# Transposes moved ahead of the first layer's matmuls, and row statistics a slot later, in an attention and MLP kernel

## The chip, the cores and the metric

The kernel runs on one core of a Trainium2 chip. The metric is the device time of one execution in microseconds. Before the change the median of three runs was 1268.01 us (1264.45 to 1271.99).

## The reference

Batch 8, 8 heads, 576 tokens, head size 64; then a two-layer perceptron of width 2048 on the 512 joined features, with layer norm and a residual.

```python
scores = scale * np.matmul(q, k.transpose(0, 1, 3, 2))      # 8 x 8 heads, 576 x 576
cum = np.cumsum(np.log(np.clip(f, 0.0001, 1.0)), axis=-1)
decay = cum[:, :, :, None] - cum[:, :, None, :]
scores = np.where(causal, -1e9, scores + decay)
attn = np.exp(scores - np.max(scores, axis=-1, keepdims=True))
attn = attn / (np.sum(attn, axis=-1, keepdims=True) + 1e-09)
x = heads_joined(np.matmul(attn, v))                        # (8, 576, 512)
xn = (x - mean(x)) / np.sqrt(var(x) + 1e-06) * g_ln
out = x + np.maximum(xn @ w_ch1, 0.0) @ w_ch2
```

## The kernel before, in words

All 64 heads are done one after the other, each in four slots, and the layers run beside them. A head's 576 query rows are cut into row tiles 0 to 4 (64 rows, then four of 128, table `QT`); the slots of a head are t = 1, 2, 3, 4, and slot t=1 does row tile 0 too. Row tile t needs 192, 320, 448 and 576 keys. There are 256 slots, numbered u. Products are made of values split into a high and a low part (names `h`/`hi` and `l`/`lo`) so that float32 accuracy comes from the fast matmul format.

In a slot the work of several stages meets, and each stage is a piece named by one letter. The string of letters in `ORDERS` is the order in which the pieces' instructions are issued; each engine runs its own instructions strictly in that order, and so does each DMA queue. The pieces that matter here:

- Q (`qk_mm`): TensorE makes the scores of row tile t, tiles `s`.
- S (`softmax_a`, L409): VectorE adds the mask and takes the row maximum, `s` to `p`. e (`softmax_e`, L420): ScalarE, exponential with row sums. B (`softmax_b`): VectorE adds and inverts the sums (L425, L426), POOL scales the rows (L427), and a DMA on SP's queue (L440) writes them to a tile `pw` of the fast format.
- t (`transpose_unit`, L446): two slots later (`LAG`) TensorE transposes `pw` into PSUM tiles `tr` (and `tr_4b` for the last columns of row tile 4). So slot t=1 transposes row tile 3 of the head before, t=2 its row tile 4, t=3 row tiles 0 and 1 of the own head, t=4 row tile 2.
- h (`transposed_hi`, L504): ScalarE copies `tr` to the high part `ph`. l (`transposed_lo`, L509): VectorE makes the low part (the instructions read `tr` and `ph`; the tile written is `pl`, or `ph` in its upper half).
- A (`av_unit`, L543): in slots t=1 and t=3, TensorE makes the product with v, tile `o`, from the `ph` and `pl` of the three slots before; the last of them were written in the slot just before. F (`finish`, L579) and a (`finish_add`, L590) take `o` out of PSUM; ScalarE does F ahead of e.
- M (`Moe.first`, `mm1`, L622 to L624): twelve matmuls of 256 columns, one sixteenth (step j) of the first layer for a chunk of 256 tokens, tile `h`. r (`mm1_high`, L630): relu on ScalarE, tile `hh`. m (`mm1_low`, L635): the low part on VectorE. N (`Moe.second`, `mm2`, L644 to L646): six matmuls of 512 columns, the second layer for the step of the slot before, into `acc`. After the last step N also calls `chunk_out` (L703, L705), which needs `rs`.
- R (`Moe.rest`): after steps j=11 and j=13 `chunk_rows` transposes 128 tokens' rows into a PSUM tile `xp`, copies them to `xt` (L669, ScalarE) and takes their mean and variance (L674, L675, VectorE); after steps 9 and 11 `rows_load` reads such rows, tile `xw`, with 4 to 8 DMAs on SP; `fetch` loads and splits the next chunk's inputs (`xr`, `x`; L655, L606, L607).
- L (`run_later`): up to six of the 14 POOL instructions by which `chunk_rstd` makes `rs`.
- P (`prep`): the next head's casts on ScalarE (L342, L348), VectorE (L349, L356) and POOL (L343, L350, L357), and the load of v (L332). D (`next_raw`): the load of a later head (L325).

All tiles of TensorE's output but `acc` take turns in six PSUM banks (`bank`). After the last slot a loop does M, r, m, L, N, R for the remaining steps alone (the tail). The third table rules slots 66 and later, the second slots 37 to 65.

Of the kernel before, what the change touches and what calls it, by code (L numbers as in the profile page):

```python
# [19 lines left out]
FT = DFF // P  # L20
# [27 lines left out]

ORDERS = [
    (0, "WwQsSthAeMrgFBmlLNPaRf"),  # L50
    (37, "WwQSstAMhPelgNFrfmBDLRa"),
    (66, "QSAFeMaBPrthNmlRLD"),
]


# [1 line left out]
def attn_moe(ctx: ExitStack, tc: tile.TileContext, qk, v, f, g, w1, w2, out):  # L57
# [13 lines left out]
    def bank(name):  # L71
        return ps.tile([P, 512], F32, tag="b", bufs=6, name=name)

    def m2(name, dt):
        return work.tile([P, 512], dt, tag="m2", bufs=11, name=name)
# [340 lines left out]
    def softmax_e(h, t):  # L416
        q0, m, w = QT[t]
        pt, st = h.p[t]
        i = len(h.s[t]) - 1
        nc.scalar.activation(pt[:m, :w], pt[:m, :w], AF.Exp, bias=st[:m, i : i + 1], scale=-1.0, accum_out=st[:m, 2:3])  # L420
# [22 lines left out]
    def tr(out_, in_):  # L443
        m = in_.shape[0]
        if in_.dtype == F32R:
            nc.tensor.transpose(out_.bitcast(F32R), in_, identr[:m, :m])  # L446
        else:
            nc.tensor.transpose(out_, in_, ident[:m, :m])
# [53 lines left out]
    def transposed_hi(h, t):  # L502
        for tp, hi, lo in h.parts:
            nc.scalar.copy(out=hi, in_=tp)  # L504

    def transposed_lo(h):
        if not h.full:
            for tp, hi, lo in h.parts:
                nc.vector.tensor_tensor(out=lo, in0=tp, in1=hi.bitcast(F32), op=ALU.subtract)  # L509
# [100 lines left out]
    def new_chunk(n):  # L610
        c = Chunk()
        c.n, c.x, c.xr, c.xt, c.j = n, [], [], [], 0
        c.acc = None
        return c

    def mm1(c):
# [41 lines left out]
    def rows_load(c, i):  # L658
        c.xw = m2(f"xw{c.n}_{i}", F32R).rearrange("p (k c) -> p k c", k=KT)
        for k in range(KT):  # L660
            tokens(c, k, c.n * C + P * i, P, c.xw[:, k, :].bitcast(F32))

    def chunk_rows(c, i):

        tp = bank(f"xp{c.n}_{i}")
        for k in range(KT):
            tr(tp[:, P * k : P * k + P], c.xw[:, k, :])
        xt = m2(f"xt{c.n}_{i}", F32)
        nc.scalar.copy(out=xt, in_=tp)  # L669
        if i == 0:  # L670
            c.sv = work.tile([P, 2, 2], F32, tag="sv", bufs=2, name=f"sv{c.n}")
            c.rs = work.tile([P, 4], F32, tag="rs", bufs=2, name=f"rs{c.n}")
        bs = work.tile([P, 6], F32, tag="bs", bufs=2, name=f"bs{c.n}_{i}")
        nc.vector.bn_stats(bs, xt)  # L674
        nc.vector.bn_aggr(c.sv[:, i, :], bs)  # L675
        c.xt.append(xt)

    later = []

    def run_later(k):  # L680
        while later and k > 0:
            later.pop(0)()
            k -= 1

    def chunk_rstd(c):

        var, y, t = c.sv[:, :, 1], c.rs[:, 0:2], c.rs[:, 2:4]
        ve = nc.gpsimd
        later.append(lambda: ve.tensor_scalar_add(var, var, 1e-6))
        later.append(lambda: ve.tensor_scalar(  # L690
            out=y.bitcast(I32), in0=var.bitcast(I32), scalar1=-0.5, scalar2=1597463007.0, op0=ALU.mult, op1=ALU.add
        ))
        for _ in range(3):
            later.append(lambda: ve.tensor_mul(t, y, y))
            later.append(lambda: ve.tensor_mul(t, t, var))
            later.append(lambda: ve.tensor_scalar(out=t, in0=t, scalar1=-0.5, scalar2=1.5, op0=ALU.mult, op1=ALU.add))
            later.append(lambda: ve.tensor_mul(y, y, t))
# [9 lines left out]
    class Moe:  # L707
# [49 lines left out]
        def rest(self):  # L757
            c, self.step = self.step, None
            if c is not None:
                self.prev = (c, c.pend)  # L760
                if c.j in (FT - 5, FT - 3):
                    chunk_rows(c, (c.j - (FT - 5)) // 2)
                if c.j in (FT - 7, FT - 5):
                    rows_load(c, (c.j - (FT - 7)) // 2)
                if c.j == FT - 3:
                    chunk_rstd(c)
            self.fetch()

        def left(self):
# [2 lines left out]
    moe = Moe()  # L772
# [7 lines left out]
    def start_head(n):  # L780
        hd[n] = load(n)
# [11 lines left out]
    for u, slot in enumerate(slots):  # L793

        def before(k):
            return slots[u - k] if u >= k else None

        if slot is not None:
            n, t = slot
            h = hd[n]  # L800
        av = None
        if before(LAG + 1) is not None and before(LAG + 1)[1] in (2, 4):
            av = hd[before(LAG + 1)[0]]
        want = moe.can(wp.ready()) and u >= FIRST_MOE

        def piece(c):
            tu = before(LAG)
            if c == "t" and tu is not None:
                transpose_unit(hd[tu[0]], tu[1])
            elif c == "h" and tu is not None:  # L810
                transposed_hi(hd[tu[0]], tu[1])
            elif c == "l" and tu is not None:
                transposed_lo(hd[tu[0]])
            elif c == "Q" and slot is not None:
                if t == 1:
                    qk_mm(h, 0)
                qk_mm(h, t)
            elif c == "A" and av is not None:
                av_unit(av, before(LAG + 1)[1])
            elif c == "S" and slot is not None:  # L820
                if t == 1:
                    softmax_a(h, 0)
                softmax_a(h, t)
            elif c == "e" and slot is not None:
                if t == 1:
                    softmax_e(h, 0)
                softmax_e(h, t)
            elif c in FILL:
                wp.fill(FILL[c])
            elif c == "s":  # L830
                wp.sums()
                if u == LAG:
                    busy(WARM[2])
            elif c == "F" and av is not None:
                finish(av)
            elif c == "a" and av is not None:
                finish_add(av)
            elif c == "r" and want:
                moe.first_high()
            elif c == "R":  # L840
                moe.limit = min(NCHUNK, max(0, u - LAG - 1) // (4 * H) * S // C)
                moe.rest()
            elif c == "L":
                run_later(RSTD)
            elif c == "M" and want:
                moe.first()
            elif c == "B" and slot is not None:
                if t == 1:
                    softmax_b(h, 0)
                softmax_b(h, t)  # L850
            elif c == "m" and want:
                moe.first_low()
            elif c == "W":
                due = 1 + min(u, W_CHANGE) / W_SLOTS + max(0, u - W_CHANGE) * W_TICKS
                while not wp.done() and wp.tick_no <= due:
                    wp.tick()
            elif c == "N":
                moe.second()
            elif c == "P":
                prep()  # L860
            elif c == "D":
                next_raw()

        def next_raw():

            if slot is not None and t in (2, 3) and NFULL <= n + 2 < B * H:
                if t == 2:
                    start_head(n + 2)
                load_raw(hd[n + 2], 1 if t == 2 else 0)

        def prep():

            if slot is not None:
                if t == 1 and n + 1 < NFULL:
                    start_head(n + 1)
                if n == NFULL - 2 and t == 1:
                    while not wp.done():
                        wp.tick()
                        wp.fill(99)
                    early.close()  # L880
                    pools["late"] = ctx.enter_context(tc.tile_pool(name="late", bufs=1))
                if n + 1 >= NFULL and n + 1 < B * H:
                    if t == 2:
                        prep_a(hd[n + 1])
                    if t == 3:
                        prep_b(hd[n + 1])
                if not h.full and t == LAG + 1:
                    prep_v(h)
                if t == LAG + 1 and n + 1 < B * H:
                    load_v(hd[n + 1])  # L890

        for c in [o for first, o in ORDERS if first <= u][-1]:
            piece(c)
    moe.limit = NCHUNK
    while moe.left() > 0 or moe.prev is not None:
        if moe.can(2 * FT):
            moe.first()
            moe.first_high()
            moe.first_low()
        run_later(RSTD)  # L900
        moe.second()
        moe.rest()
# [38 lines left out]
```

## Time and profile before

| | before |
|---|---|
| median of three runs | 1268.01 us |
| profiled execution | 1266.57 us |
| its span | 1264.8 us |
| mean granted TensorE clock | 0.991 |
| matmuls / other matmul-engine instructions | 8368 / 8368 |
| HBM read, written | 79.61 MB, 19.17 MB |

The span is the time from the first to the last instruction of one execution. Busy times are of single engines and overlap. The ends of matmuls are modelled, so that a matmul's duration includes its way through the array; how fast matmuls follow one another is read from their starts. In rows of the timeline the first number is the start from the span's begin and the second the duration, both in us; a bracket gives idle time of the engine just before and what ended it. In rows of DMA issues the last number is the median time in us from issue to landing.

### The profile page before, as it was taken

Reading aid. Unit: us, or ns where it says so; the run is one execution under the profiler, and the core shown is the slowest. Engines: PE = TensorE matmul, PEld = TensorE weight load, DVE = VectorE, ACT = ScalarE, POOL = GpSimd, SP = SyncE. Lnnn points to the kernel's source line nnn. Section 1 sums busy time; section 2 is a strip of 40 time slices with the busy share of each in tenths; the row PEclk is TensorE's granted clock in tenths of the full one; section 3 lists DMA queues with packets and bytes.
Section 4 is the critical chain, followed back from the end, with each engine's and each line's share of the span. In section 5 each row is a group of like instructions: output and inputs, shape, how many; then the busy total and the mean of one; then the engine's idle time right before and its main releaser. Section 6 shows DMA issues by size and latency. Waiting matters only on the chain.

```text
span 1264.8 us, 26082 instructions
## 1 busy us (share of the span) xinstructions
PE 1208.8 (96%) x8368; PEld 1076.5 (85%) x8368; DVE 755.6 (60%) x2664; ACT 621.9 (49%) x1936; POOL 445.6 (35%) x768
## 2 busy tenths in 40 slices
PE   8889999989899999999999999998999999999998
PEld 6657877879788888889898989887888989999997
DVE  6778773566666767676667666766766662222222
ACT  5887674545545555555555555554555542112111
POOL 3544353344434434344434344444334330000000
PEclk8999999999999999999999999999999999999999
DMA  6555442333434343434433434433343421110100
GB/s 173 155 152 167 134 112 69 100 124 120 128 124 121 125 132 117 137 126 118 133 125 128 124 129 127 136 111 114 126 120 123 141 82 39 41 44 17 51 26 26
DMA packets 129657, 139.04 MB, mean 110 GB/s; under 512 B 34544, under 2 KB 102128, under 8 KB 129520
## 3 DMA queue, kind: packets, MB, share of 16 engines
q1 hardware_dynamic: 129520, 137.37, 35.6%
q8 instruction: 67, 1.10, 0.4%
q14 instruction: 70, 0.57, 0.2%
HBM read 79.61 MB, written 19.17 MB: 78 GB/s over the span
## 4 chain that ended last, share of the span: by engine, by line
PE 67%; DVE 13%; ACT 9%; issue 4%; DMA 4%; SPq 2%; POOL 1%; DVEq 0%; POOLq 0%; ACTq 0%
PE h L622 9%; PE acc L644 8%; PE h L623 8%; PE h L624 8%; PE acc L645 8%; PE acc L646 8%; PE o L543 5%; ACT p L420 4%; DVE p L409 4%; PE tr L446 2%; PE s L374 2%; DMA pw<-p 2%; PE o L518 2%; PE s L376 2%; PE s L377 2%
## 5 line engine op out<-in xcount | busy, mean ns | idle before, releaser
L427 POOL TENSOR_SCALAR p<-p,st 64x64 f32<-64x64 f32 (+4 forms) x320 | 173.7, 544 | 542.0 <-ACT p L420 193.4
L622 PE MATMUL h<-x,w1h 128*128 128x256 f32 x1152 | 334.1, 290 | 0.4 <-DVE st L409 0.4
L623 PE MATMUL h<-x,w1h 128*128 128x256 f32 x1152 | 326.9, 284 | 0.0
L624 PE MATMUL h<-x,w1l 128*128 128x256 f32 x1152 | 326.4, 283 | 0.0
L420 ACT ACTIVATE p<-p,st 64x64 f32<-64x64 f32 (+4 forms) x320 | 179.1, 560 | 211.4 <-DVE st L409 209.2
L635 DVE SCALAR_TENSOR_TENSOR hh<-h,hh 128x256 fp32r<-128x256 f32 x288 | 121.3, 421 | 209.4 <-ACT hh L630 206.6
L644 PE MATMUL acc<-w2h,hh 128*128 128x512 f32 x576 | 242.2, 420 | 0.0
L646 PE MATMUL acc<-w2h,hh 128*128 128x512 f32 x576 | 226.6, 393 | 0.0
L645 PE MATMUL acc<-w2l,hh 128*128 128x512 f32 x576 | 226.5, 393 | 0.0
L622 PEld LDWEIGHTS h<-x,w1h 128*128 128x128 f32 x1152 | 220.2, 191 | 5.6 <-issue 0.9
L623 PEld LDWEIGHTS h<-x,w1h 128*128 128x128 f32 x1152 | 220.9, 192 | 2.5
L624 PEld LDWEIGHTS h<-x,w1l 128*128 128x128 f32 x1152 | 221.0, 192 | 0.0
L630 ACT ACTIVATE hh<-h 128x256 fp32r<-128x256 f32 x288 | 109.1, 379 | 181.7 <-PE h L624 178.2
L409 DVE CUSTOM_DVE_ANT_0 p<-s,mask 64x64 f32<-64x64 f32 (+4 forms) x320 | 133.1, 424 | 19.2 <-PE s L377 5.6
L646 PEld LDWEIGHTS acc<-w2h,hh 128*128 128x128 f32 x576 | 108.3, 188 | 25.4
L425 DVE TENSOR_SCALAR st<-st 128x1 f32<-128x1 f32 (+1 forms) x320 | 47.8, 149 | 122.0 <-ACT p L420 118.3
L644 PEld LDWEIGHTS acc<-w2h,hh 128*128 128x128 f32 x576 | 108.6, 189 | 13.7 <-ACT ph_full L504 0.2
L645 PEld LDWEIGHTS acc<-w2l,hh 128*128 128x128 f32 x576 | 109.4, 190 | 12.6
L504 ACT CAST ph<-tr 64x128 fp32r<-64x128 f32 (+4 forms) x384 | 107.2, 329 | 0.2
L579 ACT COPY ot<-o 64x320 f32<-64x320 f32 x96 | 38.0, 396 | 129.5 <-PE o L543 129.2
L543 PEld LDWEIGHTS o<-ph,vv 128*128 128x128 f32 x384 | 54.4, 188 | 44.2 <-DVE ph L509 26.9
L543 PE MATMUL o<-ph,vv 128*128 128x256 f32 (+2 forms) x384 | 61.4, 281 | 31.0 <-DVE ph L509 31.0
(89 smaller groups left out, 1928.5 us busy)
## 6 DMA issues: line engine op xcount, KB each, us to landing
raw<-in_qk_dram SPq DMA_DIRECT2D x96, 288.0 KB, 2.9
wr<-in_w_dram SPq DMA_DIRECT2D x32, 512.0 KB, 5.2
pw<-p SPq DMA_DIRECT2D x48, 288.0 KB, 3.2
pw<-p SPq DMA_DIRECT2D x48, 224.0 KB, 2.2
vr<-in_v_dram SPq DMA_DIRECT2D x64, 160.0 KB, 2.2
out_dram<-xt SPq DMA_DIRECT2D x36, 256.0 KB, 2.1
pw<-p SPq DMA_DIRECT2D x48, 160.0 KB, 2.1
xa<-xs SPq DMA_DIRECT2D x32, 160.0 KB, 1.8
```

The source lines that it names most:

```text
L409: nc.vector.tensor_tensor_reduce(out=pt[:m, a:z], in0=sp, in1=mask[:m, off + a : off + z], scale=-SCALE, scalar=3.0e38 if i == 0 else st[: ...
L420: nc.scalar.activation(pt[:m, :w], pt[:m, :w], AF.Exp, bias=st[:m, i : i + 1], scale=-1.0, accum_out=st[:m, 2:3])
L427: nc.gpsimd.tensor_scalar(out=pt[:m, :w], in0=pt[:m, :w], scalar1=st[:m, 3:4], scalar2=1.0, op0=ALU.mult, op1=ALU.mult)
L543: mm(o, st, mv, start=first, stop=True, skip_group_check=True)
L622: mm(ph, w1h[:, k, fs], c.x[k][:, 0, :], start=(k == 0), stop=False)
L623: mm(ph, w1h[:, k, fs], c.x[k][:, 1, :], start=False, stop=False)
L624: mm(ph, w1l[:, k, fs], c.x[k][:, 0, :], start=False, stop=(k == KT - 1))
L630: nc.scalar.activation(h[:, 0, :], c.ph, AF.Relu)
L635: nc.vector.scalar_tensor_tensor(out=h[:, 1, :], in0=ph, scalar=0.0, in1=h[:, 0, :].bitcast(F32), op0=ALU.max, op1=ALU.subtract)
L644: mm(c.acc[i], h[:, 0, ts_], w2h[:, j, :], start=(j == 0), stop=False)
L645: mm(c.acc[i], h[:, 0, ts_], w2l[:, j, :], start=False, stop=False)
L646: mm(c.acc[i], h[:, 1, ts_], w2h[:, j, :], start=False, stop=(j == FT - 1))
```

## The change

The third table moves t ahead of M, h ahead of P and r, and l ahead of P and m. m stands ahead of N instead of behind. The copy of `xp` and the statistics become a piece of their own, b (`rows_stats`): in the third table it stands behind m and N and ahead of R, so it works on the rows that R transposed a slot before; in the second table it stands behind R, in the same slot. `chunk_rstd` is called by it after the second half of the rows. In the tail b stands ahead of L.

```diff
     (0, "WwQsSthAeMrgFBmlLNPaRf"),
-    (37, "WwQSstAMhPelgNFrfmBDLRa"),
-    (66, "QSAFeMaBPrthNmlRLD"),
+    (37, "WwQSstAMhPelgNFrfmBDLRba"),
+    (66, "QSAFteahBlMPrmNbRLD"),
...
         for k in range(KT):
             tr(tp[:, P * k : P * k + P], c.xw[:, k, :])
+        c.rows = (i, tp)
+
+    def rows_stats(c):
+        if c is None or c.rows is None:
+            return
+        i, tp = c.rows
+        c.rows = None
         xt = m2(f"xt{c.n}_{i}", F32)
         nc.scalar.copy(out=xt, in_=tp)
...
         nc.vector.bn_stats(bs, xt)
         nc.vector.bn_aggr(c.sv[:, i, :], bs)
         c.xt.append(xt)
+        if i == 1:
+            chunk_rstd(c)
...
-                if c.j == FT - 3:
-                    chunk_rstd(c)
...
+            elif c == "b":
+                rows_stats(moe.cur)
...
             moe.first_low()
+        rows_stats(moe.cur)
         run_later(RSTD)
```

TensorE in a slot t=2 of head 22: the last matmul of M, the transposes of row tile 4, and N. Before:

```order
L624 MATMUL h_13_4451<-x_3_3611,w1l 128x256
L446 MATMUL tr_4_4476<-identr,pw_4_4344 64x128
L446 MATMUL tr_4_4476<-identr,pw_4_4344 128x128 x3
L446 MATMUL tr_4b<-identr,pw_4_4344 128x128
L644 MATMUL acc_0_3725<-w2h,hh_12_4408 128x512
L645 MATMUL acc_0_3725<-w2l,hh_12_4408 128x512
```

The same slot now, from Q (tile `s`):

```order
L376 MATMUL s_2_0_4433<-hi_4207 128x320
L377 MATMUL s_2_0_4433<-kl_4208,xq_2727 128x320
L446 MATMUL tr_4_4439<-identr,pw_4_4330 64x128
L446 MATMUL tr_4_4439<-identr,pw_4_4330 128x128 x3
L446 MATMUL tr_4b<-identr,pw_4_4330 128x128
L622 MATMUL h_13_4458<-x_0_3151,w1h 128x256
```

The transposes stand right behind Q, and the twelve matmuls of M behind them, so a transpose that waits holds up M and N.

ScalarE in a slot t=2 of head 29: exponential (L420), the cast of the next head's keys (L342), relu (L630) and the copies of the transposes (L504). Before:

```order
L420 ACTIVATE p_2_6188,st_2_6189<-p_2_6188,st_2_6189 128x320
L342 CAST hi_6210<-raw_1_5990 128x576
L630 ACTIVATE hh_9_6215<-h_9_6192 128x256
L504 CAST ph_28_6156<-tr_4_6217 64x128
L504 CAST ph_28_6156<-tr_4_6217 128x3x128
L504 CAST ph_28_6156<-tr_4b 128x128
```

The same slot now:

```order
L420 ACTIVATE p_2_6188,st_2_6189<-p_2_6188,st_2_6189 128x320
L504 CAST ph_28_6129<-tr_4_6191 64x128
L504 CAST ph_28_6129<-tr_4_6191 128x3x128
L504 CAST ph_28_6129<-tr_4b 128x128
L342 CAST hi_6223<-raw_1_5990 128x576
L630 ACTIVATE hh_9_6228<-h_9_6210 128x256
```

The copies went from behind the cast and the relu to right behind the exponential.

VectorE around the slot t=4 that follows, where rows of tokens had been transposed at the end of t=3: the statistics (BN_STATS, BN_AGGR), S (L409), B (L425, L426), m (L635) and l (L509). Before:

```order
L674 BN_STATS bs_0_6320<-xt_0_6316 128x6
L675 BN_AGGR sv_6318<-bs_0_6320 128x2
L409 ISA p_4_6339,st_4_6340<-s_4_0_6333,mask 128x288
L409 ISA st_4_6340 128x1
L409 ISA p_4_6339,st_4_6340<-s_4_1_6336,mask,st_4_6340 128x288
L409 ISA st_4_6340 128x1
L425 TENSOR_SCALAR st_4_6340<-st_4_6340 128x1
L426 RECIPROCAL st_4_6340<-st_4_6340 128x1
L635 SCALAR_TENSOR_TENSOR hh_11_6362<-h_11_6344,hh_11_6362 128x256
L509 TENSOR_TENSOR ph_29_6294<-tr_2_6364,ph_29_6294 64x128
L509 TENSOR_TENSOR pl_29_6295<-tr_2_6364,ph_29_6294 128x256
```

The same slot now:

```order
L409 ISA p_4_6332,st_4_6333<-s_4_0_6326,mask 128x288
L409 ISA st_4_6333 128x1
L409 ISA p_4_6332,st_4_6333<-s_4_1_6329,mask,st_4_6333 128x288
L409 ISA st_4_6333 128x1
L425 TENSOR_SCALAR st_4_6333<-st_4_6333 128x1
L426 RECIPROCAL st_4_6333<-st_4_6333 128x1
L509 TENSOR_TENSOR ph_29_6264<-tr_2_6336,ph_29_6264 64x128
L509 TENSOR_TENSOR pl_29_6265<-tr_2_6336,ph_29_6264 128x256
L635 SCALAR_TENSOR_TENSOR hh_11_6363<-h_11_6350,hh_11_6363 128x256
L681 BN_STATS bs_0_6376<-xt_0_6372 128x6
L682 BN_AGGR sv_6374<-bs_0_6376 128x2
```

The statistics went from the head of the slot's list to its end, and l from behind m to ahead of it.

More of the change, by code (lines that the diff above doesn't have):

```diff
@@ L612, in new_chunk @@
         c.n, c.x, c.xr, c.xt, c.j = n, [], [], [], 0
-        c.acc = None
+        c.acc = c.rows = None
         return c
```

## Prediction

> **What bounds the kernel now.** I read the page, then the busy time by stretch, then the waits by engine inside the long stretch, then the chain and the timeline at single waits. The page's first part names the engine:
>
> ```profile
> PE 1208.8 (96%) x8368; PEld 1076.5 (85%) x8368; DVE 755.6 (60%) x2664; ACT 621.9 (49%) x1936; POOL 445.6 (35%) x768
> ```
>
> The stretches (busy time of each engine, then granted clock, DMA share, GB/s) part the slots that the third order table rules (243 to 1062 us) from the tail, which holds only the layers:
>
> ```profile
> 243.00:1062.00 819.00, 785.46 (x5524) 716.17 (x5523) 543.54 (x1956) 424.46 (x1347) 329.67 (x540) 1.00 0.39 122
> 1062.00:1264.80 202.80, 198.97 (x1282) 180.17 (x1280) 49.52 (x113) 36.24 (x93) 13.71 (x70) 1.00 0.11 32
> ```
>
> TensorE is the bound in both, at a granted clock of 1.00. In the middle it is idle 819.0 - 785.5 = 33.5 us, and the waits in that stretch (total, times, longest) say for what:
>
> ```profile
> PE o L543 <- DVE ph L509: 31.0, 39, 2.4
> ...
> POOL sv L689 <- DVE sv L675: 37.2, 12, 4.3
> ```
>
> Nearly all of it is one wait: piece A, the product with v, waits for piece l, the low halves of the transposed weights, which VectorE made last in the slot before. (The second row counts chunks: 12 have their statistics in this stretch.) One such wait in the timeline, in a slot t=2 and the A of the slot t=3 behind it:
>
> ```profile
> 602.30 0.70 DVE L674 BATCH_NORM_STATS2 bs<-xt 128x6 f32<-128x512 f32 x1 [0.90 <-ACT xt L669]
> ...
> 604.19 0.19 ACT L420 ACTIVATION_READ_ACCUMULATOR p<-p,st 128x1 f32 x1
> 604.28 0.66 ACT L342 CAST hi<-raw 128x576 fp32r<-128x576 f32 x1
> ...
> 604.59 0.17 DVE L426 RECIPROCAL st<-st 128x1 f32<-128x1 f32 x1
> ...
> 604.84 0.37 ACT L630 ACTIVATE hh<-h 128x256 fp32r<-128x256 f32 x1
> ...
> 605.12 0.62 ACT L504 CAST ph<-tr 64x128 fp32r<-64x128 f32 x2
> 605.25 0.43 DVE L635 SCALAR_TENSOR_TENSOR hh<-h,hh 128x256 fp32r<-128x256 f32 x1 [0.49 <-ACT hh L630]
> 605.29 0.37 PE L377 MATMUL s<-kl,xq 66*128 66x448 f32 x1
> ...
> 605.77 0.28 DVE L509 TENSOR_TENSOR ph<-tr,ph 64x128 fp32r<-64x128 f32 x1
> 606.09 0.56 DVE L509 TENSOR_TENSOR pl<-tr,ph 128x384 fp32r<-128x384 f32 x1
> 606.11 0.80 PE L543 MATMUL o<-ph,vv 128*128 128x256 f32 x5 [0.45 <-DVE ph L509]
> ```
>
> After the exponential (ends 604.38) ScalarE casts the next head's keys, then the relu, then the transposes (605.12); VectorE makes hh's low half first (605.25) and l from 605.77. A starts at 606.11. The bracket says 0.45, but ends on TensorE are modelled: a product of 448 columns hands over after 0.2 us where nothing waits, so A was due at 605.5 and lost 0.6. From starts, not brackets, I make the 39 waits 37 us (0.16 more each), and take 37, with 31 as the lower end.
>
> **The change, part by part.**
>
> *t ahead of M, h ahead of casts and relu, l ahead of the casts and m.* No instruction is added. In the event above B ends at 604.76; l's three instructions (the two shown and 0.28 for tr_4b) would run from there to 605.9, its first done at 605.04, half a microsecond before A is due; the h that they read follows the exponential at 604.38 and takes 0.62 + 0.27. The other A slot, t=1, follows t=4, whose exponential is the longest:
>
> ```profile
> 712.12 0.78 ACT L420 ACTIVATE p<-p,st 128x576 f32<-128x576 f32 x1 [2.04 <-DVE st L409]
> ...
> 713.21 0.17 DVE L426 RECIPROCAL st<-st 128x1 f32<-128x1 f32 x1
> ...
> 714.48 0.51 PE L543 MATMUL o<-ph,vv 128*128 128x320 f32 x3
> ```
>
> l would run from 713.38 for 0.28 + 0.42, to 714.1, and A is due at 714.48: cover 0.4. So this wait goes: **-37 us** (ends -31 and -37). What takes its place in l's old room is m, now last on VectorE: it has until N of the next slot, behind Q, A, t and M, over 2 us. The cast of the next head's keys and the relu on ScalarE come 0.5 to 0.9 us later, by the h rows; the POOL subtraction behind the cast has an idle POOL (35%) after it.
>
> *Junctions of short and long matmuls.* The first long matmul behind a row of short ones loses some time:
>
> ```profile
> 711.01 0.28 PE L622 MATMUL h<-x,w1h 128*128 128x256 f32 x1
> 711.13 0.29 PE L623 MATMUL h<-x,w1h 128*128 128x256 f32 x1
> ...
> 712.45 0.37 PE L446 MATMUL tr<-identr,pw 128*64 128x128 f32 x3
> 712.65 0.46 PE L644 MATMUL acc<-w2h,hh 128*128 128x512 f32 x1
> 712.96 0.39 PE L645 MATMUL acc<-w2l,hh 128*128 128x512 f32 x1
> 713.19 0.40 PE L646 MATMUL acc<-w2h,hh 128*128 128x512 f32 x1
> ...
> 715.02 0.33 PE L622 MATMUL h<-x,w1h 128*128 128x256 f32 x1
> 715.18 0.28 PE L623 MATMUL h<-x,w1h 128*128 128x256 f32 x1
> ...
> 719.98 0.46 PE L446 MATMUL tr<-identr,pw 128*64 128x128 f32 x4
> ```
>
> Behind transposes N's first step is 0.31 instead of 0.23 (0.08 lost); behind A, M's first is 0.16 instead of 0.12 (0.04); behind Q nothing. Before, a slot with A pays both; after, t stands between A and M, so one loss of 0.08 is left: 0.04 to 0.05 in some 85 slots with A, **-4 us** (ends 0 and -9: no loss left at all in those slots).
>
> The Trainium skill, page "TensorE: Matmul & The Clock Gate", section "Back-to-back issue gap", speaks against that term: it gives about 81 ns for each sustained matmul of 128 columns with its own weights, so a longer row of short ones would cost more and the loss is not paid once a row. By it, three or four more short matmuls in the row, each 20 ns over the shortest spacing, would take the 4 us away. The trace gives 65 to 75 ns here (three transposes from 712.45 to 712.65, four in 0.30), between the two.
>
> *What the transposes now wait for.* t reads pw, which a DMA on SP brings two slots after Q. Moved ahead of M it is due 712.45 - 711.01 = 1.44 us sooner, and in t=1 the removed wait of A brings it nearer still. Shortest of the four is row tile 4, transposed in slot t=2:
>
> ```profile
> pw<-p SPq DMA_DIRECT2D x48, 288.0 KB, 3.2
> ```
>
> Landing takes 3.2 us by that row. In an ordinary head:
>
> ```profile
> 714.41 0.47 SPq L440 DMA_DIRECT2D pw<-p  x1
> ```
>
> The issue follows POOL's row, which hangs on Q through S, e and B, all in their old order; it lands at 717.6, and t came at 719.98: spare 2.4, after the change 0.9. But once a chunk rows_load puts its reads into SP's queue ahead of it:
>
> ```profile
> 594.18 0.33 SPq L332 DMA_DIRECT2D vr<-in_v_dram  x1
> 594.61 0.71 SPq L655 DMA_DIRECT2D xw<-xb  x1
> ...
> 597.30 0.56 PE L543 MATMUL o<-ph,vv 128*128 128x320 f32 x3 [0.62 <-DVE ph L509]
> ...
> 599.69 0.47 SPq L440 DMA_DIRECT2D pw<-p  x1
> ...
> 603.23 0.46 PE L446 MATMUL tr<-identr,pw 128*64 128x128 f32 x4
> ```
>
> From 594.61 to 599.69 SP issues eleven DMAs of some 0.45 us. pw lands at 602.9, t came at 603.23: spare 0.3. After, with 1.44 and A's own 0.78 gone, TensorE waits 1.9 us there, with M and N queued behind t. I did this for all 48 heads: issue, plus 3.2, against t's start, less 1.44 and less the A wait between. Ten are short, by 15.8 us together (first and last below; with each DMA's own landing instead of 3.2 it is 12 heads and 19.8):
>
> ```profile
> 258.43 0.47 SPq L440 DMA_DIRECT2D pw<-p  x1
> ...
> 264.06 0.46 PE L446 MATMUL tr<-identr,pw 128*64 128x128 f32 x4
> ...
> 1007.03 0.47 SPq L440 DMA_DIRECT2D pw<-p  x1
> ...
> 1011.85 0.46 PE L446 MATMUL tr<-identr,pw 128*64 128x128 f32 x4
> ```
>
> I take **+18 us**. The ends: +5 if SP's queue itself clears sooner and only the shift by M counts, +20 by the landings.
>
> *Statistics a slot later.* Before, the copy of xp waits for the transposes at the slot's end and the statistics for the copy (0.90 in the row of 602.30); S of the next slot stands behind. After, both inputs are long there; 0.9 us a time on VectorE, off the path once l is early, so 0. The price is PSUM: xp's bank is held until ScalarE has made the next slot's relu (0.37 above) and the copy. The rows show no such wait. Both run beside N (six steps of 0.23, 1.4 us), so the bank is free about when that slot ends; were they half a microsecond late and the bank wanted at once, 24 places would cost 12 us, and nothing where one of the other five banks is next. That is the nearer case, since a slot takes about four: 0. chunk_rstd starts a slot later, so two of its 14 POOL instructions run only when chunk_out asks; chunk_out then waits for POOL once a chunk, but m and l stand ahead of it now: 0. The second table only moves the copy behind rest in the same slot, and the tail's TensorE has 3.8 us idle in all: 0 for both.
>
> **Sum.** -37 - 4 + 18 = -23 on the profiled execution's 1266.6 (span 1264.8 and 1.8 around it): 1243.6. The median of the runs shown is 1.4 higher, so I say **1245 us**.
>
> **The rivals.**
> - *The transposes take what A gave up twice over (slower).* Place: t in slot t=2, every head, not ten. The landings of pw reach far in this stretch:
>
> ```profile
> DMA to landing us min/median/max: 1.7/2.2/4.8
> ```
>
> At 4.8 instead of 3.2 the ordinary spare of 0.9 turns into a wait of 0.7; 48 heads make 32, and the sum is +9: 1277. It decides from about 1.4 us later than now ((23 / 48) + 0.9). Against it: issue there follows Q, S, e, B, whose order stays. Chance 0.09.
> - *The wait of A stays in part (no change).* Cover for l is 0.4 to 0.5 us. If S, e and B run 0.65 later than in the rows, as they may with m and the statistics ahead of S, some 83 A's wait 0.2 each, 17 us, and the sum is -6: 1262. For it: VectorE is busy 66% there. Chance 0.15.
> - *The queue clears and nothing replaces the wait (faster still).* -37 - 4 + 5 = -36: 1232. For it: S of row tile 4 no longer stands behind statistics. Against: POOL had its row done before SP issued it, so SP is the limit. Chance 0.24.
> - The forecast, 1236 to 1256, has 0.52.
>
> The range reaches from the full gain to the partial one, 1230 to 1265. About 0.5%, 6.3 us, is what a measurement of this kernel can tell from no change. Faster 0.52 + 0.24 = 0.76, same 0.15, slower 0.09.
>
> **What would show it.** Right: A's wait for ph falls under 8 us; t (L446) waits for pw some 15 to 20 us in about a dozen places, one a chunk, always ahead of tr_4b, with xw reads ahead of pw in SP's queue; N's first step is 0.23 and M's first behind t near 0.2; the tail is as long as before. Wrong: A still waits for DVE; t waits in most heads; TensorE waits for a bank after xp; or ScalarE's later relu makes N wait.

## The result, and the profile after

The changed kernel took 1252.91 us (median of 4 runs, 1250.83 to 1254.38) against 1267.25 us for the kernel before on the same chip: a ratio of 0.9882, 95% interval 0.9847 to 0.9917. The forecast was 1245 us in a range of 1230 to 1265, so the way and the range held and the gain came out at about three fifths of what was forecast (14 us instead of 23). Run again beside other kernels it gave 0.9884 (0.9856 to 0.9913). One of the six executions of the kernel with one read of rows, below, took 6478.84 us and is left out of that kernel's numbers.

The waits of TensorE in the long stretch of the changed kernel (total, times, longest), where before A's wait stood with 31.0:

```profile
PE tr L446 <- DMA pw<-p: 18.2, 14, 2.6
PE h L622 <- DVE pl L509: 5.3, 4, 1.3
PE o L543 <- DVE ph L509: 1.5, 4, 0.4
```

A's wait is gone, t's wait for pw is there at the size forecast, and a third one, M for l, was not forecast. Stretches from the same place in the program (from the scores of row tile 3 of head 16, the first slot of the third table, to the last matmul of A; then the rest), first before, then after:

```profile
228.94:1047.00 818.06, 784.52 (x5533) 715.27 (x5531) 548.62 (x1980) 428.02 (x1360) 334.90 (x548) 1.00 0.39 123
1047.00:1264.80 217.80, 213.97 (x1381) 193.83 (x1379) 52.73 (x121) 39.42 (x101) 13.71 (x70) 1.00 0.13 35
```

```profile
231.74:1031.26 799.52, 774.08 (x5532) 709.78 (x5531) 540.98 (x1980) 427.52 (x1360) 342.09 (x548) 1.00 0.40 126
1031.26:1249.10 217.84, 213.98 (x1381) 193.85 (x1379) 52.74 (x121) 38.42 (x101) 13.61 (x70) 1.00 0.12 35
```

The tail is unchanged (217.8), the long stretch is 18.5 us shorter, and the stretch ahead of it 2.8 us longer in this execution. Of these 2.8 us, 2.3 are not the change's work: up to the first M the two programs issue the same, and that M starts at 109.0 us before and at 111.3 after. In six executions that differ in the third table alone the stretch ahead was 227.8 to 231.9 us long.

One place where t waits, in a slot t=2 of the changed kernel, in rows of SP, TensorE and VectorE:

```profile
587.89 0.33 SPq L332 DMA_DIRECT2D vr<-in_v_dram  x1
588.28 0.42 SPq L655 DMA_DIRECT2D xw<-xb  x1
...
592.12 0.38 SPq L655 DMA_DIRECT2D xr<-xa  x1
592.59 0.38 SPq L325 DMA_DIRECT2D raw<-in_qk_dram  x1
593.07 0.47 SPq L440 DMA_DIRECT2D pw<-p  x1
```

```profile
594.30 0.31 PE L377 MATMUL s<-kl,xq 66*128 66x320 f32 x1
596.86 0.48 PE L446 MATMUL tr<-identr,pw 128*64 128x128 f32 x4 [2.25 <-DMA pw<-p]
596.89 0.49 DVE L409 CUSTOM_DVE_ANT_0 p<-s,mask 128x320 f32<-128x320 f32 x1 [2.83 <-DMA pw<-p]
597.18 0.24 PE L446 MATMUL tr_4b<-identr,pw 128*128 128x128 f32 x1
597.25 0.35 PE L622 MATMUL h<-x,w1h 128*128 128x256 f32 x1
```

It is the place that the prediction worked out at 1.9 us: eight reads of token rows, then `xr`, `raw`, and only then pw. TensorE loses 2.4 us between Q's last matmul and t (2.56 from start to start, where 0.15 would be due), with M behind it. The third row holds something that the prediction had missed: S waits for the same DMA. It writes a tile `p`, of which there are three, and the one that it takes is free only when pw has been read out of it. Such waits of S come to this in the stretch:

```profile
DVE p L409 <- DMA pw<-p: 22.1, 12, 3.1
```

What S's wait costs by itself no run separates. In the first experiment below it comes to 1.1 us, S standing behind the statistics there, and the stretch is as long.

### The profile page after: what moved, and what is told of

It reads as the page before. It is cut to its first block, busy times and chain, and to the rows that moved or that the text cites. A ratio compares the mean times of both kernels' runs of the same rounds, so it can differ in the third digit from the quotient of the medians.

```text
span 1249.1 us, 26052 instructions
## 1 busy us (share of the span) xinstructions
PE 1197.9 (96%) x8368; PEld 1070.7 (86%) x8368; DVE 749.0 (60%) x2664; ACT 620.4 (50%) x1936; POOL 452.4 (36%) x768
## 4 chain that ended last, share of the span: by engine, by line
PE 81%; DVE 6%; DMA 5%; ACT 4%; issue 2%; POOL 1%; SPq 1%; DVEq 0%; POOLq 0%; ACTq 0%
PE h L622 11%; PE h L624 10%; PE h L623 10%; PE acc L644 10%; PE acc L645 10%; PE acc L646 10%; PE o L543 5%; DMA pw<-p 4%; PE tr L446 4%; PE s L376 3%; PE s L377 3%; PE s L374 2%; PE o L518 2%; DVE p L409 2%; ACT p L420 2%
## 5 line engine op out<-in xcount | busy, mean ns | idle before, releaser
L427 POOL TENSOR_SCALAR p<-p,st 64x64 f32<-64x64 f32 (+4 forms) x320 | 169.7, 532 | 542.2 <-ACT ph L504 310.0
L622 PE MATMUL h<-x,w1h 128*128 128x256 f32 x1152 | 342.3, 297 | 5.7 <-DVE pl L509 5.3
L623 PE MATMUL h<-x,w1h 128*128 128x256 f32 x1152 | 326.4, 283 | 0.0
L420 ACT ACTIVATE p<-p,st 64x64 f32<-64x64 f32 (+4 forms) x320 | 179.2, 560 | 229.0 <-DVE st L409 216.6
L635 DVE SCALAR_TENSOR_TENSOR hh<-h,hh 128x256 fp32r<-128x256 f32 x288 | 120.4, 418 | 194.9 <-ACT hh L630 194.8
L644 PE MATMUL acc<-w2h,hh 128*128 128x512 f32 x576 | 228.9, 397 | 0.0
L646 PE MATMUL acc<-w2h,hh 128*128 128x512 f32 x576 | 225.9, 392 | 0.0
L630 ACT ACTIVATE hh<-h 128x256 fp32r<-128x256 f32 x288 | 109.9, 382 | 185.0 <-PE h L624 184.6
L409 DVE CUSTOM_DVE_ANT_0 p<-s,mask 64x64 f32<-64x64 f32 (+4 forms) x320 | 132.4, 422 | 43.8 <-DMA pw<-p 22.1
L425 DVE TENSOR_SCALAR st<-st 128x1 f32<-128x1 f32 (+1 forms) x320 | 47.5, 149 | 121.0 <-ACT p L420 118.2
L504 ACT CAST ph<-tr 64x128 fp32r<-64x128 f32 (+4 forms) x384 | 107.2, 328 | 3.7 <-PE tr L446 1.4
L446 PE MATMUL tr<-identr,pw 128*128 128x128 f32 (+1 forms) x672 | 79.4, 235 | 18.3 <-DMA pw<-p 18.2
L509 DVE TENSOR_TENSOR pl<-tr,ph 128x128 fp32r<-128x128 f32 x192 | 88.0, 458 | 4.4
```

Of the source, the lines that this page charges most:

```text
L409: nc.vector.tensor_tensor_reduce(out=pt[:m, a:z], in0=sp, in1=mask[:m, off + a : off + z], scale=-SCALE, scalar=3.0e38 if i == 0 else st[: ...
L427: nc.gpsimd.tensor_scalar(out=pt[:m, :w], in0=pt[:m, :w], scalar1=st[:m, 3:4], scalar2=1.0, op0=ALU.mult, op1=ALU.mult)
L622: mm(ph, w1h[:, k, fs], c.x[k][:, 0, :], start=(k == 0), stop=False)
L623: mm(ph, w1h[:, k, fs], c.x[k][:, 1, :], start=False, stop=False)
L630: nc.scalar.activation(h[:, 0, :], c.ph, AF.Relu)
L635: nc.vector.scalar_tensor_tensor(out=h[:, 1, :], in0=ph, scalar=0.0, in1=h[:, 0, :].bitcast(F32), op0=ALU.max, op1=ALU.subtract)
```

## The experiments

The theory: l made early hides A's wait; the reads of token rows in SP's queue, once a chunk, give part of that back at t. Rivals: the gain belongs to the later statistics; t ahead of M is too soon for pw whatever SP does; t's own place makes l early. "Waits by starts" below are TensorE's lost times between starts, over the same stretch as above: for each kind of neighbouring matmuls, what a step took over the step that is usual for its kind where nothing waits.

**The new order without the later statistics.**

```diff
-    (66, "QSAFteahBlMPrmNbRLD"),
+    (66, "QSAFteahBlMPrmNRbLD"),
```

> The new order of t, h and l with the statistics again in the slot of their transposes (b right behind R). Theory (the early l removes A's wait, reads of token rows in SP's queue give part back): the order carries nearly all of it, so 1253 to 1257 us; A waits under 4 us, t waits for pw 18 to 24 us, since S of row tile 4 stands behind the statistics again. Rival (the gain is mostly the later statistics): near before, 1262 to 1267 us, with 15 us or more of waits of A left.

1248.61 us, ratio 0.9846 (0.9822 to 0.987). TensorE's waits:

```profile
PE tr L446 <- DMA pw<-p: 10.1, 14, 2.3
PE o L543 <- DVE ph L509: 6.4, 10, 1.3
PE h L622 <- DVE pl L509: 5.3, 4, 1.3
```

That is under the theory's 1253, A's wait is over the 4 that I gave, and the order alone gives as much as the whole change (the intervals overlap). The sum of the three rows is 21.8 against 25.0 in the changed kernel, and the stretch is 799.4 against 799.5 us. t did not wait longer, as I had expected, but less: where A waits, t behind it comes that much later and finds pw there. For the most part the wait only changes its place.

**The later statistics without the new order.**

```diff
-    (66, "QSAFteahBlMPrmNbRLD"),
+    (66, "QSAFeMaBPrthNmlbRLD"),
```

> The old order of t, M, h, l with b as a piece ahead of R, so only the copy of xp and the statistics come a slot later. Theory: the A waits that follow a slot with statistics shorten, some 0.8 us in 12 places, the ordinary ones of 0.5 us stay: 1258 to 1264 us, A still waits 20 us or more, t waits for nothing. Rival (the gain is mostly the later statistics): 1253 to 1256 us, A waits under 10 us.

1252.48 us, ratio 0.9892 (0.9867 to 0.9917): faster than the theory's range, and by time at the rival's edge; but A's wait is still there, as in the theory, and t, which was to wait for nothing, waits a little:

```profile
PE o L543 <- DVE ph L509: 21.0, 26, 1.5
PE tr L446 <- DMA pw<-p: 3.1, 5, 1.1
```

So in the old order the statistics ahead of S cost some 13 us; alone, each half of the change is worth about what the whole is worth. In part they remove the same waits: by starts, 23 of the 37.5 us that A loses in the kernel before are lost in the slots right behind statistics. What is left here hangs partly on the order and partly on SP's queue, as the runs with one read show.

**One read of rows instead of eight.** Bytes and places stay; SP issues 1 or 2 DMAs for 4 to 8.

```diff
-        for k in range(KT):
-            tokens(c, k, c.n * C + P * i, P, c.xw[:, k, :].bitcast(F32))
+        t = t0 = c.n * C + P * i
+        while t < t0 + P:
...
+            nc.sync.dma_start(
+                out=c.xw[:, :, t - t0 : t - t0 + w].bitcast(F32),
+                in_=src[:, o - o0 : o - o0 + w].rearrange("(k p) t -> p k t", p=P),
+            )
+            t += w
```

> The changed kernel with the token rows read by one DMA (two where a read crosses a tensor) for all four feature blocks, instead of four to eight. Theory (t waits because these reads stand ahead of pw in SP's queue): SP is free some 3 us sooner, t's waits for pw fall from 18 to under 5 us and the time to 1237 to 1243 us. Rival (t ahead of M is too soon for pw in itself, whatever SP does): t's waits stay over 14 us, 1250 to 1254 us.

Ratio 0.9656 (0.9627 to 0.9686), 1224.9 us in the median of five executions (1218.8 to 1228.1). That is 12 us beyond the theory's end, and far from the rival's. The same place in SP's queue, and t behind it, which now does not wait:

```profile
571.24 0.33 SPq L332 DMA_DIRECT2D vr<-in_v_dram  x1
571.62 0.43 SPq L665 DMA_DIRECT2D xw<-xb  x1
572.10 0.50 SPq L665 DMA_DIRECT2D xw<-xa  x1
572.64 0.50 SPq L655 DMA_DIRECT2D xr<-xa  x1
573.25 0.38 SPq L325 DMA_DIRECT2D raw<-in_qk_dram  x1
573.75 0.47 SPq L440 DMA_DIRECT2D pw<-p  x1
```

```profile
577.52 0.31 PE L377 MATMUL s<-kl,xq 66*128 66x320 f32 x1
577.67 0.46 PE L446 MATMUL tr<-identr,pw 128*64 128x128 f32 x4
577.97 0.25 PE L446 MATMUL tr_4b<-identr,pw 128*128 128x128 f32 x1
578.06 0.35 PE L622 MATMUL h<-x,w1h 128*128 128x256 f32 x1
578.25 0.28 PE L623 MATMUL h<-x,w1h 128*128 128x256 f32 x1
578.36 0.28 PE L624 MATMUL h<-x,w1l 128*128 128x256 f32 x1
```

From vr to pw it takes 2.5 us instead of 5.2. One kind of wait of TensorE is left in the stretch, a little over the 5 us that I gave:

```profile
PE tr L446 <- DMA pw<-p: 5.2, 7, 2.0
```

M's wait for l went too, though M, l and banks were not touched. In the changed kernel the waits of M come where ScalarE stands for an `xr` read that is queued behind the `xw` reads, here 3.11 us, so that everything behind it, l at the end, comes late and M finds its PSUM bank unread:

```profile
849.12 0.41 ACT L606 CAST x<-xr 128x256 fp32r<-128x256 f32 x1 [3.11 <-DMA xr<-xa]
...
852.21 0.29 DVE L509 TENSOR_TENSOR pl<-tr,ph 128x128 fp32r<-128x128 f32 x1
...
852.65 0.36 PE L622 MATMUL h<-x,w1h 128*128 128x256 f32 x1 [1.33 <-DVE pl L509]
```

All four waits of M come 3.5 us behind such a wait of ScalarE (3.1 to 4.3 us); with one read ScalarE waits for no `xr` longer than 2.1 us. It takes t's place ahead of M as well: the kernel before has four waits of ScalarE of this kind (2.5 to 4.6 us), the next kernel too (3.1 to 3.4), and in neither does M wait.

**t behind M again, h and l early.**

```diff
-    (66, "QSAFteahBlMPrmNbRLD"),
+    (66, "QSAFeMtahBlPrmNbRLD"),
```

> The changed kernel with t behind M again, but h still ahead of P and r, and l ahead of P and m, and the statistics later. Theory: pw has its 1.44 us back, so t's waits for pw go under 3 us; l ends about 3.1 us behind Q and A is due at 3.5 to 3.8, so A waits under 8 us; the 4 us of junctions come back: 1238 to 1247 us. Rival (l needs the transposes ahead of M to be early enough): A waits 20 us or more, 1255 us or over.

1240.98 us, ratio 0.9795 (0.9773 to 0.9818): the theory's place, 11 to 12 us better than the changed kernel. t still waits 4.8 us (7 times), over the 3 that I gave, and A 7.0 (8 times), so pw's 1.44 us were not quite enough; M does not wait. t's place ahead of M was no part of the gain but a cost as long as the queue was full.

**t ahead of M, h and l late.**

```diff
-    (66, "QSAFteahBlMPrmNbRLD"),
+    (66, "QSAFteMaBPrhNmlbRLD"),
```

> t ahead of M, the statistics later, but h behind P and r and l behind m as before. Theory (A's wait goes because l is made earlier on VectorE, for which t's place is neither enough nor needed): A still waits 15 us or more, t waits for pw 3 to 15 us: 1248 to 1258 us. Rival (t's place by itself makes l early enough): A waits under 6 us, 1240 to 1248 us.

1263.09 us, ratio 0.9951 (0.9933 to 0.997), 5 us over the theory's end: worse than the later statistics alone. A waits 11.2 us, under the 15 that I gave and under the 21.0 of the later statistics alone, but t waits 14.5 instead of 3.1, and M waits 5.9 for m, a wait that I had not expected. The rival is far off: t's place by itself moves TensorE's waits about and makes them longer, some 33 us in all against 25 in the later statistics alone and 13 with l early and t behind M.

**t behind M, with one read.** The table of the one before last and the read above together.

> t behind M, h and l early, statistics later, and one read of rows. Theory: with SP's queue clear t's place hardly matters: t waits under 2 us instead of 5, but the junctions cost 4 to 5 us: 1222 to 1230 us, within 6 us of the kernel with t ahead of M and one read. Rival (t behind M is better by the 12 us that it was with eight reads): 1208 to 1216 us.

1222.75 us, ratio 0.9655 (0.9627 to 0.9683), the same as with t ahead of M. The stretch is 775.1 us with 4.6 us of waits by starts, against 772.5 us with 6.8; without waits 770.5 and 765.7. So the junctions of short and long matmuls are worth 5 us for t ahead of M, and the 12 us for t behind M are gone with the queue. t waits 2.9 us in two places, over the 2 that I gave.

**The kernel before with one read.** The read alone, in the kernel before.

> The kernel before with one read of rows and nothing else. Theory: the queue cost the kernel before less, since t there came behind A's wait and M; the waits of A that follow the queue go, the ordinary ones stay (15 us or more): 1248 to 1258 us. Rival (the queue costs the same whatever the order): 27 us less than before, 1236 to 1241 us.

1253.37 us, ratio 0.9893 (0.9871 to 0.9915), as the theory had it: A still waits 25.1 us, in 40 places, none over 0.9. The queue cost the kernel before 14 us (1.07%) and the changed one twice that (0.9882 to 0.9656).

**One read, new order, statistics at once; and one read, old order, statistics later.** The table of the first experiment and that of the second, each with the read.

> The new order of t, h and l and one read of rows, with the statistics in the slot of their transposes again. Theory (with l early and SP clear, statistics ahead of S are covered): within 6 us of the kernel with one read and later statistics, 1220 to 1232 us, all waits of TensorE under 12 us. Rival (statistics ahead of S cost 0.9 us in each of their 24 places, as they seemed to in the old order): 1236 to 1250 us.

> The old order of t, M, h, l, with one read of rows and the later statistics. Theory (the ordinary wait of A, half a microsecond in each slot t=3, belongs to the order alone): A still waits 17 us or more, 1244 to 1252 us. Rival (all of A's wait came from the queue and the statistics): A under 6 us, 1226 to 1236 us.

The first: 1223.68 us, ratio 0.9656 (0.9627 to 0.9685). With l early and SP clear it makes no difference when the statistics are taken: A waits 5.6 us and t 0.7, against 0 and 5.2 with the later ones. The second: 1234.55 us, ratio 0.9739 (0.9711 to 0.9768), by time the rival's, by A's wait between theory and rival:

```profile
PE o L543 <- DVE ph L509: 12.1, 16, 0.9
```

The ordinary wait of A, which I had called half a microsecond in each slot t=3, does not exist. Of the 40 waits in the kernel before with one read, 24 stand in the slots right behind statistics (0.6 us each in t=3, 0.8 in t=1), and with the statistics later these are gone. Of the 16 that are left, 12 come once a chunk (by starts 1.05 us each, one of them 0.5), a slot behind the one in which VectorE writes a finished chunk:

```profile
601.75 1.41 DVE L720 SCALAR_TENSOR_TENSOR xt<-acc,rs,xt 128x512 f32<-128x512 f32 x2 [0.98 <-PE acc L646]
603.08 0.42 DVE L635 SCALAR_TENSOR_TENSOR hh<-h,hh 128x256 fp32r<-128x256 f32 x1
...
604.29 0.48 DVE L409 CUSTOM_DVE_ANT_0 p<-s,mask 128x320 f32<-128x320 f32 x1
...
606.87 0.28 DVE L509 TENSOR_TENSOR ph<-tr,ph 64x128 fp32r<-64x128 f32 x1
...
607.21 0.80 PE L543 MATMUL o<-ph,vv 128*128 128x256 f32 x5 [0.89 <-DVE ph L509]
```

VectorE waits 0.98 us for the last matmul of N, writes the chunk (`chunk_out`, here L720), and only then makes m and l; S of the next slot, and with it everything up to that slot's l, comes late, and A loses 1.06 us. The new order has m and l ahead of N and so ahead of that output. About 12 us of A's wait belong to the order.

The changed kernel unaltered, beside the kernels of its chip:

> The changed kernel unaltered, beside the others on their chip: 1250 to 1255 us, stretch and waits as in its first profile, t for pw 16 to 20 us. It tells by how much a profile of one kernel changes from run to run.

1251.94 us; t waits 18.9 us, M 5.6 and A 2.1. Its stretch was 805.2 us against 799.5, with 3 us more waits by starts and a granted clock of 0.99 instead of 1.00 in the stretch: a single profile's stretch is good to some 6 us.

All ratios to the kernel before:

| reads of rows | old order | old, statistics later | new, statistics at once | new, statistics later |
|---|---|---|---|---|
| four to eight | 1 | 0.9892 | 0.9846 | 0.9882 |
| one or two | 0.9893 | 0.9739 | 0.9656 | 0.9656 |

## Why the prediction was right, and where its size was off

Waits by starts in the stretch, and the rest of it:

| term | forecast | measured, before to after |
|---|---|---|
| A waits for l | -37 | 37.5 to 2.2: -35.3 |
| t waits for pw | +18 | 2.8 to 20.7: +17.9 |
| M waits for l (PSUM bank) | none | 0 to 6.0: +6.0 |
| steps without waits (junctions) | -4 | 776.4 to 768.3: -8.1 |
| small waits | none | +1 |
| stretch | -23 | 818.1 to 799.5: -18.5 |

- *l's early place: right.* A waits 1.5 us by its row, under the 8 named. That l's place and not t's brings the gain is shown by the two experiments that move one without the other (0.9795 with l early, 0.9951 with t ahead). What had made l late was seen only later: 23 us of the wait stood behind statistics and 12 behind the output of a chunk, in 23 and 12 places.
- *t's price: right in place and cause, and in its sum.* 14 waits, all of row tile 4, 18.2 us; 12 of them have reads of token rows ahead of pw in SP's queue, one a chunk; with the reads made one, 5.2. That the sum is met so closely is partly luck. Two places that the prediction's working puts at 3.3 and 3.4 us measured 1.3 each, where M had waited 1.3 shortly before, and two that it puts at nothing measured 1.3 each.
- *Junctions: right in sign, and near in size.* 5 us by the pair with one read. About 3 of the 8.1 us in the table are not junctions: the step behind A's first product takes 0.22 us where A has waited and 0.12 to 0.17 where it has not, and over the 96 A's of the stretch these steps add up to 14.6 us after, 17.4 before. The rule of the Trainium skill, page "TensorE: Matmul & The Clock Gate", section "Back-to-back issue gap", which would have taken the 4 us away, is not borne out: from one transpose of a row to the next it takes 69 ns on average before and 70 after, where that page states about 81. The row of short ones that A and t share pays once, at M's first step (0.19 from 578.06 instead of 0.12), and A's own loss is gone.
- *What failed: the step on banks and statistics, put at 0.* It looked for a bank held by `xp` and found no wait; the bank that was short was M's, behind a late l, in four places, and cost 6.0 us. The step saw pw only as what t waits for; that `p` tiles and `xr` reads hang on the same queue was left out, so S and ScalarE's casts were late too. That the statistics are worth 0 is right behind the new order (0.9846 and 0.9882 overlap; 0.9656 twice) and wrong for the old one.
- *From 18.5 to 14.* The stretch ahead of slot 66 took 2.8 us more in the profiled execution of after, which leaves 15.7 us between the two profiled executions; in its second profile it took 1.1 us less than before, with a long stretch 6 us longer. The medians stand 14.3 us apart on one chip and 17.0 on another, while by the ratios it is about 15 on both (0.9882 and 0.9884). I do not see a further cause in the traces.
- *The rivals.* None came in as a whole. Closest was the clearing queue: it did not clear by itself, but when it was cleared the time was 1225, beyond that rival's 1232.

The version that beats both kernels is the new order with one read of rows: 0.9656, with t on either side of M.

## What to carry to other kernels

When a wait is taken off the path, ask which queue feeds the next instruction in line: here the work moved ahead ran into a DMA that stood behind ten others, eight of them small reads, and merging these reads into one or two DMAs brought, on top of the change, twice what the change itself had brought. Two edits that each remove the same lateness do not add up; measure each alone, and both behind the next limit. A DMA that is late delays not only who reads its result, but also who needs the buffer that it reads from.

## What the runs showed that I had not expected

SP issues a DMA of 128 KB in about the time of one of 32 KB. The eight reads of 32 KB ahead of `xr` took 3.8 us (588.28 to 592.12), 0.48 each; the two of 128 KB that replace them took 1.0 us (571.62 to 572.64), 0.5 each. And one late DMA held two engines: TensorE, which reads what it writes, 2.25 us, and VectorE, which wants the tile that it reads, 2.83 us.
